# A fused state-space scan and GELU layer: batch 0 prepared in two parts, decays in six ScalarE loads, three masks by ScalarE and GpSimd

## The chip, the core and the metric

The kernel runs on one core of a Trainium2 chip. A core has five engines that run side by side, each working through its own list of instructions in order: TensorE (PE: matrix products, from SBUF into PSUM; PEld is its loading of weights), VectorE (DVE), ScalarE (ACT), GpSimd (POOL), and SyncE (SP), which here only issues DMAs. They wait for each other through semaphores. The metric is device microseconds of one execution, lower is better.

## The reference

First a scan over chunks, as in a state-space model, for 4 batches, 8 heads, 768 steps, head size 32 and state size 16:

```python
log_a = np.log(np.clip(a, 1e-06, 1.0))
for c in range(nc):                          # chunks of 32 steps
    cum = np.cumsum(la, axis=-1)
    L = np.exp(cum[:, :, :, None] - cum[:, :, None, :]) * causal
    M = np.einsum('bhin,bhjn->bhij', Cc, Bc) * L
    y[:, :, sl] = np.einsum('bhij,bhjd->bhid', M, xc) \
        + np.einsum('bhin,bhnd->bhid', Cc, state) * np.exp(cum)[:, :, :, None]
    state = decay_full * state + sum_j(Bc_j * xc_j * np.exp(cum[:, :, -1:] - cum)_j)
```

Then y, as 3072 tokens of 256 features, goes through two products with the tanh form of GELU between them: `out = gelu(y @ w_in) @ w_out`, w_in being 256x2048 and w_out 2048x256.

## The kernel before

The scan is done in 24 chunks of 128 steps (6 for each batch) instead of 32 steps; the result is the same. With r_j, the product of the decays after step j in its chunk, B is multiplied by r and C by 1/r, so that the decay matrix L needs no exponentials: what is left of it is the triangular mask. Chunks are worked in units: chunk 0, chunk 1, and then pairs.

For one unit the steps are these, with the names that the code and the profile use:

- **head, per batch**: clip the decays, scan them backwards for r, transpose r, take 1/r, multiply B and C (`bc`), transpose the products so that head and state lie on the partitions (`bh`, `ch`), and mask C into even and odd heads (`ce`). `pend` holds each chunk's total decay.
- **gram, `f_G`** (line 659): four products of 32 rows per chunk give C·B into `gb`, the four PSUM banks that all units share.
- **mask, `f_M`** (line 669): VectorE multiplies 128x1024 of `gb` by the triangle into `m`, one instruction for each chunk (two half ones for chunk 0).
- **`f_D`** (680): the chunk's contribution to the state, from x and `bn` (B with steps on the partitions again); **`f_S`** and **`f_SP`** (730, 737) on VectorE update the state and spread it by heads (`sp_new`).
- **`f_Y`** (702, 711): y of the unit, in the PSUM bank `yb`; **`f_yev`** (720) moves it to `xm` as bf16.
- **`f_s1`** (757): w_in products into a ring of two PSUM tiles `hp`, 512 columns at a time; **`f_gelu`** (765) on ScalarE moves each to `gT`.
- **`f_s2`** (774): w_out products into the PSUM bank `o_ps`, **`f_oev`** (781, 783) evicts, **`f_store`** (787) stores. The last chunk is split into two column halves (`f_s2h`, 792) in two banks of `gb`, evicted by VectorE and ScalarE.

Batch 0 has a head of its own, which is what the kernel starts with. Its decays come in two loads of 64 rows by 384 steps. Chunk 0 is prepared by itself, from separate small loads of its B and C (`bc0`; line 320), by a TensorE transpose of r (483), two multiplies (576) and two TensorE transposes (583). Chunks 1 to 5 follow from loads of the whole batch (326): 24 small TensorE products (492) transpose r, two multiplies of 768 (595), twelve TensorE transposes (604), ScalarE evictions (458) and VectorE masks (619). For batches 1 to 3 loads and VectorE transposes do it (503 to 553), and six TensorE transposes per batch (625) with a ScalarE eviction of 768 columns (458) make `bn`.

The weights come as fp32 in eight loads of 512 KB (450, 454) and are cast to bf16 by GpSimd and VectorE (460, 462). Their loads, those of x and those of the other batches all are issued by SyncE, in one order, ahead of and between the stores.

The order of instructions on each engine is not written by hand. Every step is a node with an engine, an assumed duration, what it depends on and which ring buffers it takes. A planner (`run_order`) plays these through, picks at each engine the ready node with the lowest priority number (the table `PRIO` gives one for every node), and writes the program in that order. Where it sees TensorE idle before the first w_out product, it puts in matmuls on zeros (`idle`, line 1065), which keep TensorE's clock up; their number is fixed in the program. At run time each engine follows its list in order, whatever the times then are.

Of the kernel before, what the change touches and what calls it, by code (L numbers as in the profile page):

```python
# [31 lines left out]
def run_order(nodes, pools, hop=0.08, same=0.04, idle=None, wait=()):  # L32
# [64 lines left out]
    'f_clip(0, 256)': 308.538, 'f_R(0,)': -15.941, 'f_clip(256, 384)': -339.826, 'f_RT0()': 1159.49,  # L97
    'f_R(1,)': 367.141, 'f_recip0()': -323.896, 'f_mul0(1,)': -323.906, 'f_mul0(0,)': -35.176,
    'f_T0(1,)': 1123.21, 'f_T0(0,)': 1159.5, 'f_ce0()': -138.371, 'f_bh0()': 266.725, 'f_R(2,)': 330.337,
    'f_G(0,)': -91.981, 'f_pe()': -193.992, 'f_RT()': 1125.27, 'f_M(0, 0, 0, 2)': -285.936,  # L100
    'f_M(0, 0, 2, 4)': 367.131, 'f_pp()': 1125.26, 'f_recip()': 468.131, "f_castx(0, 'ACT')": 266.715,
    'f_mul(1,)': -194.002, 'f_pend()': 270.364, 'f_Y(0,)': 1119.78, 'f_yev(0,)': 209.42,
    'f_mul(0,)': -35.176, 'f_T(1,)': 1152.81, "f_wi(0, 0, 2, 'POOL')": 97.158,
    "f_E(0, 1, 'ACT', 21, 64)": 270.354, 'f_T(0,)': 55.447, "f_E(0, 1, 'ACT', 64, 128)": 272.36,
    'f_F(0, 128, 384)': 468.121, 'f_D(0,)': 1170.19, 'f_s1(0, 0)': 1244.43,
    "f_E(0, 0, 'ACT', 21, 64)": -152.035, 'f_F(0, 384, 768)': -343.397, "f_wi(1, 0, 2, 'POOL')": 106.043,
    "f_E(0, 0, 'ACT', 64, 128)": 102.425, 'f_S(0, 0)': -318.328, 'f_G(1,)': 1209.63, 'f_SP(0,)': -323.654,
    'f_gelu(0, 0)': 267.9, 'f_N(0,)': 1123.2, "f_castx(1, 'POOL')": 106.053, 'f_M(1, 0, 0, 4)': -287.074,
    'f_s1(0, 1)': 1244.44, "f_bn(0, 'ACT')": 270.405, 'f_D(1,)': 1119.09, 'f_gelu(0, 1)': 103.579,
    'f_G(2,)': 379.65, "f_wi(2, 0, 1, 'POOL')": -96.227, "f_wi(2, 1, 2, 'DVE')": 244.836,  # L110
    'f_S(1, 0)': 509.234, 'f_Y(1,)': 1167.76, 'f_SP(1,)': -318.348, 'f_s1(0, 2)': -68.513,
    'f_yev(1,)': -185.791, "f_wi(3, 0, 1, 'POOL')": 97.168, "f_wi(3, 1, 2, 'DVE')": -166.728,
# [140 lines left out]
def kernel(  # L253
# [20 lines left out]
    d_ff = moe_w_in.shape[1]  # L274
    d_model = moe_w_in.shape[0]
    n_tokens = batch * S
    NF = d_ff // 128
    UNITS = [[0], [1]] + [[c, c + 1] for c in range(2, NCH, 2)]
    NU = len(UNITS)

# [85 lines left out]
    for t in rr.values():  # L366
        nc.vector.memset(t[:, Q - 1:Q], 1.0)
# [735 lines left out]
```

## Time and profile before

| | us |
|---|---|
| three timed runs | 120.53, 119.59, 119.94 (median 119.94) |
| the profiled execution | 118.98 |
| its span, first to last instruction | 117.0 |
| busy: PE, DVE, ACT, POOL | 111.7, 71.2, 75.3, 18.1 |
| mean granted TensorE clock | 0.995 of full speed |
| fill matmuls (line 1065) in the span | 75, 8.9 us busy |

"Busy" sums the instructions of an engine; TensorE's are pipelined, so that its busy time overlaps itself and says little of what limits it. A line of the timeline gives start, duration, engine, source line, operation, output and inputs, and behind it in brackets the idle time before it with what ended it. A line of the chain gives start, duration and what the last-ending chain of work went through. The profiled execution is one run and the timed ones are others, so a sum of durations is made against 118.98 and its 117.0.

In the head, from 0 to about 20 us, all engines and the DMA are busy in turns: the windows from 4 to 24 us have a DMA share of 0.92 to 1.17. Afterwards TensorE alternates between w_in and w_out products.

### The profile page before, as it was taken

How to read it: one execution, taken by the hardware profiler on the slowest of the kernel's cores; microseconds unless marked ns; L12 is line 12 of the kernel's file. 1: busy time of each engine (PE TensorE's matmuls, PEld its weight loads, DVE VectorE, ACT ScalarE, POOL GpSimd, SP SyncE). 2: the span in 40 equal slices, each digit the busy share in tenths (PEclk: the TensorE clock that was granted, in tenths of full speed). 3: DMA queues.
4: the chain of work that ended last, by engine and by line, in shares of the span. 5: the costliest groups of instructions: out<-in, count | busy, mean ns of one | idle time of the engine just before them, and what ended most of it. 6: DMA issues, size and time to landing. Idle time of an engine off the chain costs nothing.

```text
span 117.0 us, 3536 instructions
## 1 busy us (share of the span) xinstructions
PE 111.7 (96%) x1484; PEld 98.9 (85%) x1484; DVE 71.2 (61%) x161; ACT 75.3 (64%) x145; POOL 18.1 (16%) x38
## 2 busy tenths in 40 slices
PE   5899999999999999999999999999999999999980
PEld 5788778997987897998989899898989899999970
DVE  3787999939699996994999693291919000000100
ACT  4123756795765778687666859667777776676610
POOL 7303735640032003200510000000000000000000
PEclk9999999999999999999999999999999999999998
DMA  2998979968959497579611101101101101111111
GB/s 49 251 287 233 364 180 375 313 153 188 207 137 218 112 210 169 117 186 208 172 46 45 44 7 45 41 12 45 50 0 45 50 0 44 45 50 45 46 47 45
DMA packets 44251, 14.28 MB, mean 122 GB/s; under 512 B 39052, under 2 KB 42700, under 8 KB 44236
## 3 DMA queue, kind: packets, MB, share of 16 engines
q1 hardware_dynamic: 43148, 13.95, 48.4%
q10 hardware_dynamic: 1088, 0.11, 0.7%
q8 instruction: 11, 0.18, 0.6%
q14 instruction: 4, 0.03, 0.1%
HBM read 10.91 MB, written 3.15 MB: 120 GB/s over the span
## 4 chain that ended last, share of the span: by engine, by line
PE 87%; DVE 7%; POOL 2%; issue 1%; ACT 1%; POOLq 0%; DVEq 0%; ACTq 0%
PE hp L757 35%; PE o_ps L774 31%; PE gb L659 3%; PE yb L774 3%; DVE m L669 3%; PE yb L711 3%; PE yb L702 3%; PE o_ps L1065 2%; PE gb L792 2%; DVE ce L619 1%; PE hp L492 1%; PE gb L625 1%; DVE sp_new L737 1%; DVE w_in_sb L462 1%; PE hp L680 1%
## 5 line engine op out<-in xcount | busy, mean ns | idle before, releaser
L765 ACT ACTIVATE gT<-hp 128x512 bf16<-128x512 f32 x96 | 53.6, 596 | 20.0 <-PE hp L757 19.9
L757 PE MATMUL hp<-xm,w_in_sb 128*128 128x256 bf16 (+1 forms) x416 | 53.0, 267 | 0.0
L757 PEld LDWEIGHTS <-w_in_sb 128*128 128x128 bf16 x416 | 42.0, 115 | 3.3 <-issue 2.1
L774 PE MATMUL o_ps<-w_out_sb,gT 128*128 128x256 bf16 x336 | 44.4, 273 | 0.0
L774 PEld LDWEIGHTS <-gT 128*128 128x128 bf16 x368 | 35.8, 98 | 3.6
L669 DVE TENSOR_TENSOR m<-gb,tri 128x1024 bf16<-128x1024 f32 (+1 forms) x25 | 28.5, 1171 | 0.0
L783 DVE COPY o_sb<-o_ps 128x256 f32<-128x256 f32 x1 | 0.4, 425 | 18.5 <-ACT gT L765 18.5
L781 ACT ACTIVATE o_sb<-o_ps 128x256 f32<-128x256 f32 x20 | 7.7, 386 | 4.9 <-ACT gT L765 3.2
L737 DVE SCALAR_TENSOR_TENSOR sp_new<-s_new,pend,bmask 128x256 bf16<-128x256 f32 x20 | 10.3, 526 | 0.3
L1065 PE MATMUL o_ps<-wz 128*128 128x128 bf16 x75 | 8.9, 281 | 1.3 <-DVE warm L364 1.3
L460 POOL CAST x<-xs_t 128x512 bf16<-128x512 f32 x9 | 5.6, 654 | 27.6 <-DMA xs_t<-in_x_dram 18.1
L730 DVE SCALAR_TENSOR_TENSOR s_new<-s_new,pend,hp 128x64 f32<-128x64 f32 x16 | 4.5, 279 | 7.3 <-PE hp L680 4.4
L720 ACT ACTIVATE xm<-yb 128x512 bf16<-128x512 f32 (+1 forms) x13 | 7.3, 563 | 2.4 <-PE yb L711 2.2
L1065 PEld LDWEIGHTS <-wz 128*128 128x128 bf16 x75 | 6.9, 129 | 1.6 <-DVE warm L364 1.3
L711 PE MATMUL yb<-m,x 128*32 128x128 bf16 x192 | 6.3, 223 | 0.0
L702 PE MATMUL yb<-ce,sp_new 128*32 128x128 bf16 x160 | 5.3, 221 | 0.0
L659 PE MATMUL gb<-ce,bh 32*128 32x256 bf16 x96 | 5.2, 282 | 0.1
L533 DVE TENSOR_TENSOR bc<-bc_t,rr 128x192 bf16<-128x192 f32 x12 | 4.6, 435 | 1.0 <-DMA bc_t<-in_C_dram 0.9
L460 POOL CAST w_in_sb<-wf 128x512 bf16<-128x512 f32 x6 | 3.7, 636 | 8.4 <-DMA wf<-in_moe_w_in_dram 8.4
L460 POOL CAST w_out_sb<-wf 128x1024 bf16<-128x1024 f32 x4 | 4.2, 1040 | 2.4 <-DMA wf<-in_moe_w_out_dram 2.4
L711 PEld LDWEIGHTS <-x 128*32 128x32 bf16 x192 | 3.8, 97 | 0.8 <-issue 0.8
L702 PEld LDWEIGHTS <-sp_new 128*32 128x32 bf16 x160 | 2.9, 96 | 1.7 <-issue 1.6
(83 smaller groups left out, 67.3 us busy)
## 6 DMA issues: line engine op xcount, KB each, us to landing
out_dram<-o_sb SPq DMA_DIRECT2D x23, 128.0 KB, 1.8
xs_t<-in_x_dram SPq DMA_DIRECT2D x3, 768.0 KB, 6.6
wf<-in_moe_w_in_dram SPq DMA_DIRECT2D x4, 512.0 KB, 7.0
wf<-in_moe_w_out_dram SPq DMA_DIRECT2D x4, 512.0 KB, 6.4
bc_t<-in_B_dram SPq DMA_DIRECT2D x12, 96.0 KB, 2.8
bc_t<-in_C_dram SPq DMA_DIRECT2D x12, 96.0 KB, 2.3
x_t<-in_x_dram SPq DMA_DIRECT2D x6, 128.0 KB, 7.3
bc_t<-in_C_dram SPq DMA_DIRECT2D x1, 384.0 KB
```

Of the source, the lines that this page charges most:

```text
L460: nc.gpsimd.tensor_copy(out=o, in_=i)
L659: nc.tensor.matmul(out=gb[:, g, 256 * k:256 * k + 256], lhsT=bh_of(gc)[32 * g:32 * g + 32], rhs=ce_of(gc)[32 * g:32 * g + 32], start=True, ...
L669: nc.vector.tensor_tensor(out=MT[gc][:, g0:g1], in0=gb[:, g0:g1, 256 * k:256 * k + 256] .rearrange("p g (e t) -> p g e t", e=2), in1=tri_b ...
L702: nc.tensor.matmul(out=y4[32 * j:32 * j + 32, k, w], lhsT=sp[:, 32 * h:32 * h + 32], rhs=ce_of(gc)[:, h % 2], start=first(j), stop=False, ...
L711: nc.tensor.matmul(out=y4[32 * j:32 * j + 32, k, w], lhsT=X16[u][:, k, 32 * h:32 * h + 32], rhs=m[:, h // 2, h % 2, :], start=first(j), st ...
L720: nc.scalar.activation(xm[:, :, t0:t0 + n * Q].rearrange("p w (c t) -> p c w t", c=n), y4[:, 0:n], AF.Copy)
L737: nc.vector.scalar_tensor_tensor(out=sp_new.rearrange("p (g d) -> p g d", g=4), in0=state[("s", gc)].rearrange("p (o d) -> p o d", o=1).to ...
L757: nc.tensor.matmul(out=hp[:, j * nt:(j + 1) * nt], lhsT=w_in5[:, kc, fi // 4, fi % 4], rhs=xm[:, kc, t0:t0 + nt], start=(kc == 0), stop=(k ...
L765: nc.scalar.activation(gts[u][:, i * per:(i + 1) * per, 0:nt], hps.pop((u, i)).rearrange("p (j t) -> p j t", j=per), AF.Gelu_apprx_tanh)
L774: nc.tensor.matmul(out=ops[gc], lhsT=gts[u][:, fi, tt * Q:(tt + 1) * Q], rhs=w_out_sb[:, fi, :], start=(fi == 0), stop=(fi == NF - 1), ski ...
L781: nc.scalar.activation(o_sb, ops.pop(gc), AF.Copy)
L1065: nc.tensor.matmul(out=zb[:, 0:128], lhsT=wz[:, 0:128], rhs=wz[:, 0:128], start=True, stop=True)
```

## The change

What it does, part by part:

- **Loads of batch 0.** The decays come by chunk, in six loads of 32 rows x 128 steps that ScalarE issues first of all. B and C come in two parts, chunks 0 and 1 and chunks 2 to 5, each part as one load for B and one for C, with no separate load for chunk 0. x comes by chunk, all six of batch 0 ahead of w_out.
- **Head of batch 0.** Both parts go the same way: clip, scan, a VectorE transpose of r, 1/r, four multiplies for each part (B and C, heads 0 to 3 and 4 to 7), products with the identity into fp32 PSUM (line 597), evictions that are masks for C (ScalarE with a scale, or VectorE) and copies for B, TensorE transposes for `bn` and their evictions. The products that transposed r are gone. `par`, `selq` and `mq` are reductions of the identity on VectorE.
- **Masks of chunks 1, 3 and 5.** ScalarE copies the 128x1024 tile of `gb` to `m` (line 694) and GpSimd sets what lies off the triangle to zero in place (697).
- **`bn` of batches 1 to 3.** The six TensorE transposes and the ScalarE eviction are replaced by two regrouping copies for each batch (`bq`, most on GpSimd) and four DMAs from SBUF to SBUF (645).
- **Order and engines.** A table `ENG` now names the engine for copies that several engines can do, so that some evictions of y and of the output and some casts move to VectorE. w_in products of chunks 0 and 1 may alternate, and chunk 1's w_out products go to the other half of chunk 0's PSUM bank, alternating with chunk 0's. `PRIO` is a new table.
- **Last chunk.** Its halves lie in the two tiles of the ring `hp` instead of two banks of `gb`.

```diff
@@ loads and head of batch 0
-    nc.sync.dma_start(out=a_t[0:32], in_=a_half[0])
-    nc.scalar.dma_start(out=a_t[32:64], in_=a_half[1])
-    load_bc0(1, nc.sync)
-    load_bc0(0, nc.scalar)
+    A0 = [(0, 2), (2, CPB)]
+    NP = [32 * (c1 - c0) for c0, c1 in A0]
...
+    def load_a0(c):
+        k = int(c >= A0[1][0])
+        o = 32 * (c - A0[k][0])
+        nc.scalar.dma_start(
+            out=a0t[k][o:o + 32],
+            in_=bass.AP(tensor=a.tensor, offset=a.offset + c * Q, ap=[[S, 32], [1, Q]]))
+
+    def load_bc0(k, i):
+        c0, c1 = A0[k]
+        src = (B, C)[i]
+        nc.sync.dma_start(out=bcq[k][:, i],
+                          in_=bass.AP(tensor=src.tensor, offset=src.offset + c0 * Q * N,
+                                      ap=[[R * N, NP[k]], [S * N, H], [1, R * N]]))
...
+    for c in range(CPB):
+        load_a0(c)
...
+    def f_clip0(k):
+        nc.vector.tensor_scalar(out=a0c[k], in0=a0t[k], scalar1=1e-6, scalar2=1.0, op0=ALU.max, op1=ALU.min)
...
+    def f_mul0(k, i, h0, h1):
+        nc.vector.tensor_tensor(
+            out=bq16(k)[:, i, :, h0:h1], in0=bcq[k][:, i, h0:h1].rearrange("p h (r n) -> p r h n", r=R),
+            in1=(r0T_of(k), q0T[k])[i][:, :, h0:h1].rearrange("p r (h o) -> p r h o", o=1)
+            .to_broadcast([NP[k], R, h1 - h0, N]), op=ALU.mult)
+
+    def f_T0(k, i):
+
+        n = NP[k]
+        T0[(k, i)] = t = next_hp()[:, 0:R * n]
+        for r in range(R):
+            nc.tensor.matmul(out=t.rearrange("q (p r) -> q r p", r=R)[:, r],
+                             lhsT=bq16(k)[:, i, r].rearrange("p h n -> p (h n)"),
+                             rhs=ident[0:n, 0:n], start=True, stop=True)
...
+        if eng == "ACT":
+            nc.scalar.activation(o, i, AF.Copy, scale=par[:, e:e + 1])
+        else:
+            nc.vector.tensor_scalar(out=o, in0=i, scalar1=par[:, e:e + 1], scalar2=None, op0=ALU.mult)
@@ bn of batches 1 to 3
-    def f_N(b):
-        U[b]["n"] = (gb[:, 1] if b else next_hp())[:, 0:S // 2].bitcast(BF16)
-        for c in range(1 if b == 0 else 0, CPB):
-            nc.tensor.transpose(out=U[b]["n"][:, c * 128:(c + 1) * 128],
-                                in_=U[b]["bh"][:, c * Q:(c + 1) * Q], identity=ident)
...
+    def load_bn(b, g):
+
+        d = U[b]
+        if "bn" not in d:
+            d["bn"] = next_bn()
+        nc.sync.dma_start(out=d["bn"][:, 192 * g:192 * g + 192],
+                          in_=d["bq"][32 * g:32 * g + 32].rearrange("p r c n -> p r (c n)"))
@@ masks
+    BYPOOL = range(1, 6, 2)
...
+    def f_MA(u, k):
+
+        gc = UNITS[u][k]
+        MT[gc] = next_m()
+        nc.scalar.activation(MT[gc], gb[:, :, 256 * k:256 * k + 256].rearrange("p g (e t) -> p g e t", e=2), AF.Copy)
+
+    def f_MP(gc):
+        nc.gpsimd.affine_select(out=MT[gc], in_=MT[gc], pattern=[[0, 4], [0, 2], [1, Q]],
+                                compare_op=ALU.is_ge, fill=0.0, base=0, channel_multiplier=-1)
...
+            elif gc in BYPOOL:
+                ma = add("ACT", 1.0, f_MA, u, k, deps=[gn], prio=q + 1)
+                mp = add("POOL", 1.38, f_MP, gc, deps=[ma], prio=q + 1)
@@ last chunk
     def f_s2h(h):
+        ops[("h", h)] = next_hp()[:, 0:128]
...
-            nc.tensor.matmul(out=gb[:, 2 * h, 0:128], lhsT=gts[NU - 1][:, f, Q:2 * Q],
+            nc.tensor.matmul(out=ops[("h", h)], lhsT=gts[len(BLOCKS) - 1][:, f, Q:2 * Q],
```

In the order that the planner makes of it, TensorE's list has 105 fill matmuls instead of 75: 24 at first, then groups of 10, 6, 7, 11, 3, 11 and 11 between the steps of the head, 8 before the first w_in group, and groups of 1 and 5 between the eight w_in groups of chunks 0 and 1. The last one stands behind the eighth of these. On VectorE the last of the second part's multiplies stands behind chunk 1's state update and ahead of chunk 0's masks; on GpSimd chunk 1's select stands behind the casts of x for chunks 0 and 1 and ahead of all casts of weights. In the head of batch 1 all four multiplies of C now come ahead of the first transpose, where two did before, and the stores of chunks 0 and 1 stand between SyncE's DMAs for batch 1's `bn`.

## The prediction

> **What bounds the kernel now.** I read the busy lines first, then the chain that ended last, then the windows of the fill matmuls (line 1065, which multiply zeros only to keep TensorE at work), then the head's timeline engine by engine.
>
> ```profile
> PE 111.7 (96%) x1484; PEld 98.9 (85%) x1484; DVE 71.2 (61%) x161; ACT 75.3 (64%) x145; POOL 18.1 (16%) x38
> PE 87%; DVE 7%; POOL 2%; issue 1%; ACT 1%; POOLq 0%; DVEq 0%; ACTq 0%
> ```
>
> TensorE is busy nearly always and carries 87% of the chain. But part of that is fill:
>
> ```profile
> 0.00:12.00 12.00, 6.48 (x50) 5.21 (x50) 1.00 0.88 209
> 12.00:20.00 8.00, 2.11 (x23) 1.50 (x24) 1.00 0.96 300
> 20.00:30.00 10.00, 0.28 (x2) 0.14 (x2) 1.00 0.91 223
> 30.00:60.00 30.00, 0.00 (x0) 0.00 (x0) 1.00 0.82 169
> ```
>
> These are the windows of line 1065 (busy of PE and PEld with counts, granted clock, DMA share, GB/s). After 20.3 us there is no fill and the clock is 1.00: from there TensorE works through a fixed list. So the end is "when does the last fill end" plus "how much real TensorE work is left", unless a later wait opens. The pieces of the chain that mark this:
>
> ```profile
> 20.21 0.11 PE o_ps L1065 x2
> 32.49 0.35 PE gb L659 x8
> 111.77 1.80 PE gb L792 x32
> 113.66 0.30 DVE o_sb L462
> 114.03 0.28 ACT o_sb L458
> ```
>
> The last fill ends at 20.32, the first gram matmuls of batch 1 (chunks 6 and 7) start at 32.49, the last matmul ends at 113.57, and 3.43 us of eviction and store follow to 117.0. From 20.32 to 113.57 is 93.25 us.
>
> That gram is no free point. VectorE's timeline shows what releases it:
>
> ```profile
> 30.75 0.64 DVE L533 TENSOR_TENSOR bc<-bc_t,rr 128x192 bf16<-128x192 f32 x2 [0.92 <-DMA bc_t<-in_C_dram]
> 31.42 0.38 DVE L543 STREAM_TRANSPOSE ch<-bc 128x192 f32<-128x192 f32 x1
> 31.84 0.55 DVE L553 TENSOR_SCALAR ce<-ch,pari 128x192 int32<-128x192 int32 x2
> ```
>
> VectorE waited 0.92 us for batch 1's C, then scaled, transposed and masked it until 32.39; TensorE took it 0.1 us later. So the load of C is as late as TensorE there: a shorter head alone would wait at this place.
>
> **The change, part by part.**
>
> *TensorE's list.* In the order of the changed kernel the last fill stands right after the eighth w_in group of chunks 0 and 1. What is left there is less than at 20.32 of before: one such group (0.57, "L757 x8"), the Y of chunks 2 and 3 (0.56) and three batches of six transposes (line 625, 0.34 each, replaced by DMAs): 2.15 us. So the end is the same if the last fill ends near 22.5, at equal stalls.
>
> *The head's chain.* I walk it with the rows of before. Six loads of the decays of 0.42 to 0.45 us issue each on ScalarE's queue run from 0.80 to 3.4, the table load (1.28) then ends at 4.7, and ScalarE's first use is after 5. The two loads of the first part land by 3.2 to 3.3 (a_t took 1.9 from issue). VectorE has its constants by about 3.05 (three reductions sized from the 0.255 of line 394, the copy of 0.37 of line 397, one cast of the identity). Clip 0.2, scan 0.42, transpose 0.43 and the state factor 0.15 end at 4.5. Multiplies of 256 elements are not in the trace; between 0.28 (128) and 0.95 (768) a line gives 0.42. Four of them, a reciprocal of 0.37 (between 0.21 for 8 and 0.46 for 48), one copy of 0.28 and a 0.24 end at 7.1; TensorE transposes, ScalarE scales four pieces at 0.28 to 8.7, chunk 1's gram starts at 8.6. ScalarE's copy of its mask tile, 128x1024 from PSUM, is not in the trace: 0.384 (256) and 0.596 (512) give 1.02, so 9.05 to 10.1. GpSimd's select of 1024: 0.292 (128) and 0.450 (256) give 1.38, so 10.2 to 11.6. On VectorE the second part's clip, scan, transpose, factor, three multiplies, a state copy and a reciprocal bring 10.2, a state update 10.5; the last multiply is then due beside the select.
>
> What happens to a VectorE instruction beside GpSimd can be read off:
>
> ```profile
> 15.05 0.42 DVE L462 CAST w_in_sb<-wf 128x512 bf16<-128x512 f32 x1
> 15.99 0.65 POOL L460 CAST w_in_sb<-wf 128x512 bf16<-128x512 f32 x1 [1.50 <-DMA wf<-in_moe_w_in_dram]
> 16.09 0.83 DVE L462 CAST w_in_sb<-wf 128x512 bf16<-128x512 f32 x1
> 20.11 1.04 POOL L460 CAST w_out_sb<-wf 128x1024 bf16<-128x1024 f32 x1 [0.30 <-DMA wf<-in_moe_w_out_dram]
> 20.31 1.12 DVE L737 SCALAR_TENSOR_TENSOR sp_new<-s_new,pend,bmask 128x256 bf16<-128x256 f32 x1
> ```
>
> The cast takes 0.42 alone and 0.83 beside GpSimd, the sp update 0.48 alone (28.26) and 1.12: both end 0.28 after GpSimd's instruction (16.64 and 21.15). So the multiply ends at 11.88 instead of 10.9. Then: two half masks of chunk 0 (1.29) to 13.2, a scaled piece 0.43, sp 0.48, a copy 0.35 to 14.4; D and Y of chunk 1 to 15.05; eight fills to 15.55. From there each pair of w_in groups is a round trip over two PSUM tiles: 0.66 from matmul to gelu, 0.60 gelu, 0.2 back (17.00 to 17.64 to 18.29), 1.46 for a pair; three pairs, 0.6 for a cast of x on ScalarE and one group more: the last fill ends near 21.75. The first w_out product waits for a cast on VectorE (it stands behind chunk 4's mask, from 20.4, 1.2, then 0.42) to 22.1. Weights arrive in time in this walk: 768 KB of x stand ahead of w_out instead of 512, 128 KB fewer of B and C are read, so net 128 KB, 0.5 us at the windows' 250 to 300 GB/s: w_in's last quarter at 16.5 (15.99 before), w_out's first at 19.3 (18.76).
>
> *From there to chunk 6's gram.* 88 matmuls of 0.109 and one Y, 10.1 us, and 0.3 of latencies as before: 32.5. VectorE's side: all six x of batch 0 now stand ahead too, so the same bytes less 128 KB precede C: landing near 30.2. But all four multiplies (1.3) now precede the first transpose (0.38) and masks (0.55): 32.45, 32.55 on TensorE. Both sides meet; I take 32.55 against 32.49.
>
> *After it.* Four w_in matmuls more and four w_out matmuls fewer are done by then, which cancels; two sets of transposes are gone, 0.68. 81.08 becomes 80.4: the last matmul ends at 112.95. The masks of chunks 1, 3 and 5 and the bn evictions moved to or off ScalarE cost nothing here: its idle after 32 us is mostly "gelu waits for PE", 19.9 in all. GpSimd sits idle for 9.5 to 9.9 at a time, which covers the new regrouping copies.
>
> *The tail.* Before, ScalarE's last copy stood behind VectorE's, both in one tile: 114.03, 0.46 after the last matmul. Now the halves have tiles of their own, and ScalarE's needs only about the 0.2 seen from matmul to eviction: 0.25 less.
>
> Sum: 32.55 - 32.49 - 0.68 - 0.25 = -0.87 us. The profiled execution took 118.98 us for a span of 117.0; the sum gives 118.1. The three timed runs have the median 119.94, 0.96 above it; on that scale the forecast is **119.1**. Differences under 1% (1.2 us) hardly count here.
>
> Not shown in the trace: the DMAs from SBUF to SBUF that replace the transposes (below 0: a load that lands ahead costs nothing; above: 2.8 us, the landing of a B load, if all of it is waited for; I take 0, as the copies end near 30.5 and D of chunk 6 is due at 35.7, with four issues of 0.5 and two stores between). The select beside VectorE: from 0 (it does not block) to the 1.4 of its length; I take the 0.95 of one blocked multiply, by the casts' rows. ScalarE's copy of 1024: 0.8 (the bn row of 768) to 1.2.
>
> The Trainium skill, "SBUF — State Buffer", section "Who interferes with whom", says that VectorE with two SBUF inputs, or in its two-port modes, shares a port pair with GpSimd under an exclusive lock, and that the one which comes second blocks for the whole instruction. The two ends at +0.28 agree; no row here shows a select in that place. It speaks against this change, which puts three long selects and more copies beside such VectorE work; taken for every overlap it gives the first rival's time.
>
> **Rivals.**
>
> 1. *VectorE behind GpSimd, everywhere (slower).* Beside the one multiply, three more weight casts on VectorE (+0.42 each) and two or three sp updates (+0.3 to 0.64) stand beside GpSimd's casts and selects between 12 and 20 us: 1.3 + 1.2 = 2.5. It decides once chunk 2's mask ends after 19.5, for then gram 4/5 and the last pair are late: last fill 24.2, end +2.4: 121.5. For: rows above; VectorE is busy 3.9 of 4 us in 12 to 20. Against: masks from PSUM took 1.22 and 2.34 beside GpSimd as without.
> 2. *Nothing blocks and C comes early (faster).* The multiply goes ahead of the select: 0.95 less, last fill 20.8; 1024 fewer small packets let C land at 29.3. Gram at 31.6: 118.2. For: DMA is the limit there, share 0.8 to 1.2. Against: C needs both.
> 3. *C lands as before (the transfer decides).* At 30.75 the gram is at 33.2 whatever the head gains: 119.8. That the change moves only the head, and not the time, is this case.
> 4. *The DMAs for bn are late.* They queue behind two stores that wait for evictions, and GpSimd's copies block on VectorE's multiplies. If the last lands at 38 instead of 35, TensorE stands 2.3 us: 121.4.
>
> **Chances.** Forecast 0.36 (118.5 to 119.6), rival 1 0.15, rival 2 0.22, rival 3 0.17, rival 4 0.10. Faster by over 1% (below 118.74): rival 2 and the forecast's lower third, 0.34. Slower (above 121.14): most of rivals 1 and 4, 0.22. Within: 0.44. The range reaches from rival 2 with the tail's gain doubled and chunk 0's walk 0.5 shorter, 117.4, to rival 1, 121.5.
>
> **What would show it.** Last fill near 21.8; the first mask of chunk 0 right behind a select at 11.6 to 11.9; a VectorE wait for C near 30.2 and gram 6/7 at 32.5; no line of 625's kind after 32; the last copy 0.2 after the last matmul. Wrong: the last fill beyond 23, TensorE gaps between 32 and 60, or the D of chunk 6 released by a DMA.

## The result: slower, and the profile after

| | before | after |
|---|---|---|
| timed runs, median (us) | 120.23 (119.59 to 120.62) | 124.87 (124.50 to 126.77) |
| ratio after/before, 95% interval | | 1.0384 (1.0323 to 1.0446) |
| the profiled execution, and its span | 118.98, 117.0 | 126.77, 125.0 |
| gram of chunks 6 and 7 | 32.49 | 34.55 (forecast 32.55) |
| from it to the last matmul's end | 81.08 | 87.40 (forecast 80.4) |
| from there to the end of the span | 3.43 | 3.05 (forecast 3.18) |

The forecast was 119.1, with a range of 117.4 to 121.5: wrong, in sign too. Ratios, here and below, are to the kernel before, timed beside it, with 95% intervals, and leave out runs that were disturbed on either side, so they need not be the quotient of two medians. The profiled execution is the longest of the four. A second profiled execution of the same kernel (124.84 us, span 123.0) is set beside it where that matters: TensorE ran at half clock for some 3.4 us in both, and what the first has more is mostly longer stands of TensorE (4.66 us after 34 us, against 3.04).

The page of the changed kernel: busy lines, and the engines' shares of the chain that ended last.

```profile
PE 114.0 (91%) x1475; PEld 100.0 (80%) x1475; DVE 72.8 (58%) x176; ACT 75.7 (61%) x147; POOL 19.8 (16%) x38
PE 74%; DVE 8%; DMA 7%; SPq 4%; ACT 3%; issue 1%; ACTq 0%; DVEq 0%
```

TensorE's share of the chain fell from 87% to 74%. DMA (7%) and SyncE's queue (SPq, 4%) are new in it. No engine became the bound; TensorE waits for transfers. The windows of the fill matmuls (now line 1135: busy of PE and PEld with counts, granted clock, DMA share, GB/s):

```profile
0.00:12.00 12.00, 7.62 (x61) 6.11 (x61) 1.00 0.74 160
12.00:20.00 8.00, 3.67 (x37) 2.81 (x37) 1.00 0.99 288
20.00:30.00 10.00, 0.88 (x7) 0.52 (x7) 1.00 1.05 251
30.00:60.00 30.00, 0.00 (x0) 0.00 (x0) 0.94 0.72 147
```

The head is longer (seven fills after 20 us instead of two), and in the first 12 us the DMA moved 160 GB/s instead of 209, which is 0.6 MB less. The clock of 0.94 in the last row is that half clock. TensorE's timeline holds what "equal stalls" in the prediction left out (in brackets: idle time before, and what ended it):

```profile
23.86 0.22 PE L1135 MATMUL o_ps<-wz 128*128 128x128 bf16 x1
...
34.55 0.40 PE L675 MATMUL gb<-ce,bh 32*128 32x256 bf16 x8
...
38.56 0.20 PE L706 MATMUL hp<-x,bn 128*32 128x64 bf16 x1 [0.76 <-DMA bn<-bq]
39.20 0.23 PE L706 MATMUL hp<-x,bn 128*32 128x64 bf16 x5 [0.44 <-DMA bn<-bq]
...
42.36 0.30 PE L728 MATMUL yb<-ce,sp_new 128*32 128x128 bf16 x8 [1.29 <-DVE sp_new L762]
...
53.91 1.35 PE L802 MATMUL o_ps<-w_out_sb,gT 128*128 128x256 bf16 x8 [2.17 <-DVE o_sb L485]
```

Last fill at 24.08 (forecast 21.75), gram at 34.55, and then three stands: 1.20 us at the D of chunk 6, 1.29 at the Y behind it, 2.17 at a w_out group. The second and the third name VectorE, but VectorE was itself waiting. Its timeline:

```profile
41.43 0.23 DVE L495 TENSOR_SCALAR at<-at 128x128 f32<-128x128 f32 x1 [3.62 <-DMA at<-in_a_dram]
41.57 0.22 DVE L753 COPY s_new<-hp 128x64 f32<-128x64 f32 x1
41.82 0.48 DVE L762 SCALAR_TENSOR_TENSOR sp_new<-s_new,pend,bmask 128x256 bf16<-128x256 f32 x1
...
50.24 0.43 DVE L485 CAST x<-xs 128x512 bf16<-128x512 f32 x1 [2.06 <-DMA xs<-in_x_dram]
52.42 0.23 DVE L495 TENSOR_SCALAR at<-at 128x128 f32<-128x128 f32 x1 [1.75 <-DMA at<-in_a_dram]
...
53.47 0.39 DVE L485 COPY o_sb<-o_ps 128x256 f32<-128x256 f32 x1
```

At 41.43 it is the clip of batch 2's decays that waited 3.62 us, and the state copy and `sp_new`, which TensorE needs at once, stand behind it in VectorE's order. At 50.24 and 52.42 it is x of batch 2 and the decays of batch 3; the eviction that TensorE waits for stands behind both. Behind all three stands are DMAs that SyncE issued late. Its timeline (a duration here is the time that issuing took):

```profile
28.72 1.77 SPq L399 DMA_DIRECT2D xs<-in_x_dram  x1
30.59 3.91 SPq L812 DMA_DIRECT2D out_dram<-o_sb  x1
34.59 1.28 SPq L645 DMA_DIRECT2D bn<-bq  x2
35.97 0.54 SPq L812 DMA_DIRECT2D out_dram<-o_sb  x1
36.56 1.19 SPq L645 DMA_DIRECT2D bn<-bq  x2
37.80 0.59 SPq L383 DMA_DIRECT2D at<-in_a_dram  x1
```

The output of that first store had been evicted by 30.24, and yet its issue lasted until 34.50. Only then came `bn`, and the decays of batch 2 at 37.80. The same view of the kernel before:

```profile
27.28 0.47 SPq L353 DMA_DIRECT2D xs_t<-in_x_dram  x1
27.86 5.19 SPq L787 DMA_DIRECT2D out_dram<-o_sb  x2
33.10 0.58 SPq L337 DMA_DIRECT2D at<-in_a_dram  x1
```

There too the queue stood for 5 us behind the load of x (4.71 of the 5.19 us are the first store's, whose output had been evicted by 25.48), but what stood in it were stores that nobody waits for, and the decays went out 4.7 us earlier.

### The profile page after: what moved, and what is told of

Read it like the earlier page. It is cut to its first block, busy times and chain, and to the rows that moved or that the text cites. A ratio compares the mean times of both kernels' runs of the same rounds, so it can differ in the third digit from the quotient of the medians.

```text
span 125.0 us, 3564 instructions
## 1 busy us (share of the span) xinstructions
PE 114.0 (91%) x1475; PEld 100.0 (80%) x1475; DVE 72.8 (58%) x176; ACT 75.7 (61%) x147; POOL 19.8 (16%) x38
## 4 chain that ended last, share of the span: by engine, by line
PE 74%; DVE 8%; DMA 7%; SPq 4%; ACT 3%; issue 1%; ACTq 0%; DVEq 0%
PE hp L782 30%; PE o_ps L802 27%; PE o_ps L1135 4%; DMA at<-in_a_dram 3%; PE yb L802 3%; PE gb L675 3%; PE yb L728 2%; DMA a0t<-in_a_dram 2%; DVE sp_new L762 2%; SPq L645 2%; PE yb L737 2%; DMA wf<-in_B_dram 2%; DVE m L685 1%; PE hp L818 1%; ACT gT L790 1%; SPq L812 1%
## 5 line engine op out<-in xcount | busy, mean ns | idle before, releaser
L802 PE MATMUL o_ps<-w_out_sb,gT 128*128 128x256 bf16 x336 | 46.1, 276 | 2.2 <-DVE o_sb L485 2.2
L685 DVE TENSOR_TENSOR m<-gb,tri 128x1024 bf16<-128x1024 f32 (+1 forms) x22 | 25.3, 1164 | 0.1
L1135 PE MATMUL o_ps<-wz 128*128 128x128 bf16 x105 | 12.2, 283 | 1.3 <-DVE warm L408 1.3
L1135 PEld LDWEIGHTS <-wz 128*128 128x128 bf16 x105 | 9.4, 130 | 1.9 <-DVE warm L408 1.3
L481 ACT ACTIVATE o_sb<-o_ps 128x256 f32<-128x256 f32 x16 | 6.2, 385 | 5.9 <-PE o_ps L802 4.5
L485 DVE COPY o_sb<-o_ps 128x256 f32<-128x256 f32 x5 | 2.1, 417 | 9.6 <-PE o_ps L802 9.6
L481 ACT ACTIVATE xm<-yb 128x512 bf16<-128x512 f32 (+1 forms) x10 | 5.6, 556 | 1.5 <-PE hp L706 1.3
L483 POOL COPY bq<-bc 128x384 bf16<-128x384 bf16 x5 | 2.6, 527 | 21.4 <-DVE bc L528 21.4
L697 POOL TENSOR_SCALAR_AFFINE_SELECT m<-m 128x1024 bf16<-128x1024 bf16 x3 | 3.5, 1172 | 6.9 <-ACT m L694 6.9
L706 PE MATMUL hp<-x,bn 128*32 128x64 bf16 x80 | 3.3, 199 | 1.2 <-DMA bn<-bq 1.2
```

The lines of the kernel that those rows point to most:

```text
L481: nc.scalar.activation(o, i, AF.Copy)
L685: nc.vector.tensor_tensor(out=MT[gc][:, g0:g1], in0=gb[:, g0:g1, 256 * k:256 * k + 256] .rearrange("p g (e t) -> p g e t", e=2), in1=tri_b ...
L697: nc.gpsimd.affine_select(out=MT[gc], in_=MT[gc], pattern=[[0, 4], [0, 2], [1, Q]], compare_op=ALU.is_ge, fill=0.0, base=0, channel_multip ...
L802: nc.tensor.matmul(out=ops[gc], lhsT=gts[v][:, fi, tt * Q:(tt + 1) * Q], rhs=w_out_sb[:, fi, :], start=(fi == 0 and gc != 1), stop=(fi == ...
L1135: nc.tensor.matmul(out=zb[:, 0:128], lhsT=wz[:, 0:128], rhs=wz[:, 0:128], start=True, stop=True)
```

## The experiments

Theory A: the loss is made from 34 us on, by SyncE's queue: `bn` and batch 2's loads stand behind the load of batch 1's x, VectorE and TensorE behind them. Theory B: the loss is the later head. Each variant is the changed kernel with the order of all other instructions kept. Where a diff says `move`, one entry of the planned order is put behind another one.

### e0_after: the changed kernel again

> The changed kernel as it is, for a profile that can be set beside the variants. Both theories: 124.5 to 125.2 us. Theory A (the loss is made between 32 and 56 us, by SyncE's order of DMAs) expects to see TensorE stand at the D of chunk 6 (1.2 us, for bn), at the Y behind it (1.3, for sp_new) and at the first w_out group near 54 (2.2, for o_sb), 4.7 us in all; theory B (the loss is the later head, 2.0 to 2.3 us up to the gram of chunks 6 and 7) expects those stands to be peculiar to the first trace and the gram of chunks 6 and 7 near 34.5 again.

Ratio 1.0475 (1.0334 to 1.0616), from two runs. Gram of chunks 6 and 7 at 34.27, last matmul's end 85.77 later. The stands are there again: 1.05 and 0.44 at the D, 1.55 at w_out. At the Y there was none, because TensorE came late to it: it had run at half clock since 39.8. The stands are no accident of the first trace. The late gram is there again too, which is what theory B expects; this run does not tell the theories apart by the time.

### e1_early_a: the decays of batches 2 and 3 loaded early

```diff
+    move("load_a(2,)", "load_a(1,)")
+    move("load_a(3,)", "load_a(2,)")
```

> The decays of batches 2 and 3 (64 KB each) are loaded right behind those of batch 1, ahead of the stores and of the DMAs for bn, and nothing else is changed. Theory A: VectorE no longer waits 3.6 us for batch 2's decays near 41 nor 1.75 for batch 3's near 52, so TensorE's stands of 1.3 (sp_new) and 2.2 (o_sb) go: 3.5 less, 121.0 to 122.0 us. The stand of 1.2 at the D of chunk 6 stays. Theory B: TensorE is late from the head on and VectorE's waits lie beside it: 124.5 to 125.0, or 0.2 more for 128 KB ahead of batch 1's C.

Ratio 1.0294 (1.0217 to 1.0372), 123.71 us: 1.2 us less, not 3.5. VectorE's waits for decays were gone, as expected, and with them TensorE's stand at the Y; the one at w_out was 0.97. But in the profiled run (125.40 us, the longest of the five) B and C of batch 1, which now stand behind the decays, came late: SyncE issued C from 29.12 instead of 23.09, VectorE waited 3.01 us for B, TensorE 2.13 for `ce`, and the gram of chunks 6 and 7 moved to 37.54. One late load had been put in the place of another.

### e2_bn_gpsimd: the bn DMAs on GpSimd's queue

```diff
-        nc.sync.dma_start(out=d["bn"][:, 192 * g:192 * g + 192],
+        nc.gpsimd.dma_start(out=d["bn"][:, 192 * g:192 * g + 192],
```

> The twelve DMAs for bn are issued by GpSimd behind its regrouping copies instead of by SyncE between the stores. Theory A: the D of chunk 6 no longer waits for bn (1.2 less), and SyncE issues batch 2's decays 2.5 us earlier (35.3 instead of 37.8), which cuts VectorE's wait of 3.6 to 1.1 and takes most of the 1.3 at the Y: 2.0 to 2.5 less in all, 122.0 to 122.7 us. If what holds SyncE is the store ahead (3.9 us up to 34.5) and not the bn DMAs, only 1.2 goes: 123.4. Theory B: 124.5 to 125.

Ratio 1.0187 (1.0100 to 1.0274), 122.14 us: 2.7 less, as theory A had it. The stand at the D is gone and the one at the Y is 0.54; the third is still there with 2.3. The gram stayed at 34.66. By the ratios about half of the loss goes by changing who issues twelve small DMAs.

### e10_stores_last: what holds the queue

```diff
+    move("f_store(1,)", "load_a(2,)")
+    move("f_store(0,)", "f_store(1,)")
```

> The changed kernel, with the stores of chunks 0 and 1 moved in SyncE's order from among the four bn DMAs to behind the load of batch 2's decays; bn and decays stay on SyncE. It tells apart what holds bn. If it is the stores' waits for evictions (rival 4 as predicted): bn goes out when GpSimd's copies end, near 32.8, and the decays at 35.3, as with bn on GpSimd's queue: 2.0 to 2.7 us less, 122.2 to 122.9. If it is the load of batch 1's x (768 KB in 6144 pieces of 128 bytes), behind which SyncE can issue nothing until about 34.5, whatever comes next: bn is then the one that is held, goes out at 34.5 to 37.0 and the decays follow at 37.0 instead of 37.9: 0.5 to 1.2 less, 123.7 to 124.4.

Ratio 1.0389 (1.0303 to 1.0475), 125.83 us: no gain at all, and so neither of the two times expected. The order of events was that of the second alternative. SyncE's timeline of this kernel, with the first bn DMA cut out of its group by a narrow window:

```profile
29.93 1.53 SPq L399 DMA_DIRECT2D xs<-in_x_dram  x1
32.68 2.77 SPq L645 DMA_DIRECT2D bn<-bq  x1
37.44 0.59 SPq L383 DMA_DIRECT2D at<-in_a_dram  x1
```

GpSimd's second regrouping copy ended at 32.65, so nothing that the program waits for was missing. Still the issue of this one DMA took 2.77 us, until 35.45, when the x load issued at 29.93 (6.8 us to landing) had a good microsecond left. Whatever stands behind that load is held, be it a store or `bn`. The mechanism that rival 4 named, stores waiting for evictions, is not what holds it. Which limit in the queue it is, the traces do not show. The gain of 0.5 us or more did not come because the decays went out only 0.36 earlier (37.44 instead of 37.80), and in this trace the head was later (gram at 35.44) and the third stand longer (3.25).

### e3_bn_pe and e11_bn_pe: bn by TensorE, as before

```diff
+    def f_N(b):
+        U[b]["n"] = t = next_hp()[:, 0:S // 2].bitcast(BF16)
+        for c in range(CPB):
+            nc.tensor.transpose(out=t[:, c * 128:(c + 1) * 128],
+                                in_=U[b]["bh"][:, c * Q:(c + 1) * Q], identity=ident)
+    put("N1", lambda: f_N(1), "f_G(4,)")
+    put("bn1", lambda: f_bn(1), "f_gelu(3, 2)")
...
```

In e3 the transposes of batches 2 and 3 fell into a PSUM tile that a state update had yet to read, so those updates worked on other values and e3 computes something else; e11 places them two or three steps later.

> bn of batches 1 to 3 comes as in the kernel before, from six TensorE transposes per batch and one ScalarE copy of 768 columns; the two regrouping copies and the four DMAs per batch are gone. TensorE has 3 times 0.34 = 1.0 us more of work. Theory A: the stand at the D of chunk 6 goes (1.2), SyncE is 2.5 us ahead, which takes most of the 1.3 at the Y: 1.5 less net, 123.0 us. Theory B: nothing was lost by the DMAs, so the transposes cost their 1.0: 125.5 us.

> The changed kernel, with bn of batches 1 to 3 by six TensorE transposes each and a ScalarE copy of 768 columns, as in the kernel before; no regrouping copies and no DMAs for bn; all else as changed, batch 2's and 3's decays on SyncE too. TensorE has 1.0 us more of work. Theory A (the bn DMAs are late and make SyncE late): 122.3 to 123.0, in spite of that 1.0. Theory B (the loss is in the head): 125.5 to 126.

e3: ratio 1.0207 (1.0128 to 1.0287). e11: 1.0230 (1.0175 to 1.0285), 122.89 us. Theory A's number in both: giving TensorE 1.0 us more of work makes the kernel 2 us faster. The part of the change that was to save 0.68 us cost about 2 net.

### e4_two_fixes: bn and the late decays on GpSimd's queue

```diff
-        nc.sync.dma_start(out=d["bn"][:, 192 * g:192 * g + 192],
+        nc.gpsimd.dma_start(out=d["bn"][:, 192 * g:192 * g + 192],
@@ load_a
-        nc.sync.dma_start(out=at[b], in_=bass.AP(tensor=a.tensor, offset=a.offset + b * H * S - K0[b] * Q,
+        (nc.sync if b == 1 else nc.gpsimd).dma_start(out=at[b], in_=bass.AP(tensor=a.tensor, offset=a.offset + b * H * S - K0[b] * Q,
@@ order
+    move("load_a(2,)", "f_wo(3, 0)")
+    move("load_a(3,)", "load_a(2,)")
```

> The bn DMAs issued by GpSimd, and with them the loads of the decays of batches 2 and 3, issued by GpSimd behind its last weight cast; the rest as changed. Theory A: the stands that the first of these left (0.5 at the Y for sp_new, 2.3 at w_out for o_sb, both behind VectorE's waits for decays) go too: 122.1 - 2.8 = 119.3 us; the gram of chunks 6 and 7 stays at 34.0 to 34.7, and from there to the last matmul 80.4 to 81 us, as forecast. Theory B (the stands lie beside a TensorE that is late anyway): 122.1.

Ratio 0.9997 (0.9944 to 1.0050): the whole loss is gone within the noise, without a change in the head. With 120.95 us, beside a kernel before that had 120.70 in these rounds, it is 1 us or more short of the 119.3 expected: a wait of 2.93 us on VectorE for batch 2's x (47.48) was left, and with it 1.29 of the stand at w_out.

### e12_head_only: the head mended, the queue not

```diff
-            for _ in range(n):
+            for _ in range(n + (10 if t0 < 2 else 0)):
+    move("f_mul0(1, 1, 4, 8)", "f_mul0(1, 1, 0, 4)")
```

> The changed kernel with only its head mended: ten more fill matmuls before the first state factor, and the last multiply of the second part ahead of chunk 1's state update. SyncE's list is as changed. Theory A (SyncE's queue behind the load of batch 1's x decides from 34 us on): the first w_in group comes 1 to 2 us earlier, but the load of x goes out near 28.8 and batch 2's decays near 37.8 as before, so TensorE stands longer at the D of chunk 6 and the Y: 124.3 to 124.9. Theory B (the head is the loss): 1.5 to 2.0 less, 123.0.

Ratio 1.0318 (1.0250 to 1.0387), 124.44 us: 0.4 less, theory A's number. Batch 2's decays went out at 37.48, and the stands were 0.8, 1.3 and 1.7. But the test is weaker than meant. In the profiled run the head was not earlier: the first w_in group began at 16.75, against 17.97 and 16.16 in the two traces of the changed kernel, then the granted clock fell (0.74, 0.50 and 0.91 in the windows of 2 us from 16 on), the last fill ended at 24.10 and the gram of chunks 6 and 7 came at 34.57. What speaks against theory B is above all e4, which left the head alone and lost the loss.

### e13_evict_act: the eviction and the cast off VectorE

```diff
+    seq[pos("f_oev(5,)")][1] = lambda: f_oev(5, "ACT")
+    seq[pos("f_castx(7,)")][1] = lambda: f_castx(7, "POOL")
```

> The changed kernel, with the eviction of chunk 5's output on ScalarE instead of VectorE and the cast of chunks 12 and 13's x on GpSimd instead of VectorE, both at their places in the order; loads as changed. If the third stand (1.6 to 3.3 us at w_out near 53) comes about because the eviction stands on VectorE behind a cast that waits for x and a clip that waits for decays: it goes, 1.5 to 2.5 less, 122.5 to 123.4. If TensorE would stand there anyway, for the gram or the Y that need the same late loads: the stand only moves to a later line, 124.5.

Ratio 1.0247 (1.0186 to 1.0307), 123.22 us: 1.6 less. VectorE still waited 3.95 us for batch 3's decays there (51.07), but the eviction no longer stood behind. What is left of the third stand, on TensorE:

```profile
52.42 1.07 PE L782 MATMUL hp<-xm,w_in_sb 128*128 128x256 bf16 x8 [0.85 <-DVE s_new L755]
```

So this stand had two causes in series, the late loads and the table `ENG` that put a cast and an eviction on VectorE behind them. The prediction did not look at the second.

### e5_two_loads, e6_fills, e7_masks_dve: parts of the head, on e4

```diff
@@ e5: load_a0 (n is the number of chunks of the part)
-        nc.scalar.dma_start(
-            out=a0t[k][o:o + 32],
-            in_=bass.AP(tensor=a.tensor, offset=a.offset + c * Q, ap=[[S, 32], [1, Q]]))
+        if o == 0:
+            nc.scalar.dma_start(
+                out=a0t[k],
+                in_=bass.AP(tensor=a.tensor, offset=a.offset + c * Q, ap=[[Q, n], [S, 32], [1, Q]]))
@@ e6: idle
-            for _ in range(n):
+            for _ in range(n + (10 if t0 < 2 else 0)):
@@ e7: f_MA (and f_MP issues nothing)
-        nc.scalar.activation(MT[gc], gb[:, :, 256 * k:256 * k + 256].rearrange("p g (e t) -> p g e t", e=2), AF.Copy)
+        nc.vector.tensor_tensor(out=MT[gc], in0=gb[:, :, 256 * k:256 * k + 256]
+                                .rearrange("p g (e t) -> p g e t", e=2), in1=tri_b, op=ALU.mult)
```

> On the kernel with the two fixes (bn and late decays issued by GpSimd), the decays of batch 0 come in two ScalarE loads (64 and 128 rows) instead of six. In the program each of the DMAs of SyncE and ScalarE waits for the one eight places before it; with six decay loads and two of B and C in front, the first load of x is the ninth and waits for a decay load to land (2.5 us), and so on. Theory C (this makes the whole stream of loads late, 0.6 MB behind the kernel before at 12 us): x goes out at 1.7 instead of 2.5 and the first w_in load at 5.0 instead of 5.9, the gram of chunks 6 and 7 comes 0.7 to 1.0 earlier than with six loads, and the time is 0.7 to 1.0 less. Theory D (the head is late by TensorE's clock and the chain of steps): clip starts 0.5 earlier at most, nothing else moves: 0 to 0.3 less.

Ratio 1.0123 (1.0038 to 1.0208): slower than e4. The two loads take the place of six, but the first lands later. VectorE's first clip in e4, then in e5:

```profile
3.83 0.22 DVE L553 TENSOR_SCALAR a0c<-a0t 64x128 f32<-64x128 f32 x1 [1.20 <-DMA a0t<-in_a_dram]
```

```profile
4.71 0.22 DVE L555 TENSOR_SCALAR a0c<-a0t 64x128 f32<-64x128 f32 x1 [2.09 <-DMA a0t<-in_a_dram]
```

It therefore tells nothing between theories C and D.

> On the kernel with the two fixes, ten more fill matmuls in the first group (34 instead of 24), which close TensorE's gap of 0.9 us before the first state factor (4.0 to 4.9 us). Theory D (TensorE's matmuls take twice as long until 5, 9 or 13 us, by chance from run to run, because of that gap): fills of 0.06 us from about 5.5 us on in every run, steps of the head 1 to 2 us earlier, and the time 1 to 2 us less and steadier. Theory C (w_out's and C's landing decides when TensorE goes on): the head's first part is earlier, but TensorE then waits for casts of w_out and for ce, and the gram of chunks 6 and 7 and the time gain 0.5 or less.

Ratio 0.9939 (0.9894 to 0.9983), the fastest version here and the only one with an interval below 1. In this trace the rate changed as theory D said: eleven fills took 1.28 us start to start in the first trace after and take 0.72 here. These are their rows, first of the changed kernel, then of e6, each with the gram that follows them:

```profile
9.71 1.35 PE L1135 MATMUL o_ps<-wz 128*128 128x128 bf16 x11
10.99 0.40 PE L675 MATMUL gb<-ce,bh 32*128 32x256 bf16 x4
```

```profile
8.07 0.79 PE L1135 MATMUL o_ps<-wz 128*128 128x128 bf16 x11
8.79 0.29 PE L675 MATMUL gb<-ce,bh 32*128 32x256 bf16 x4
```

Chunk 1's gram came 2.2 us earlier than in the first trace after, and the last fill ended at 22.2. But the gram of chunks 6 and 7 stood at 34.58, where TensorE waited 1.0 for `ce`, and the gain over e4 is 0.6%, theory C's number, with intervals that overlap. That the gap was the reason for the slow matmuls is not shown: of the traces with the same ten more fills, e8, e12 and e14 have them slow again behind the first state factor (ten fills in 1.25 us, against 0.73 in e6 and e9). The time was not steadier either: e6's runs lie between 119.22 and 123.27.

> On the kernel with the two fixes, the masks of chunks 1, 3 and 5 are done by VectorE in one step of 1.24 us at the place where ScalarE's copy stood; no copy and no select. If the selects hurt (VectorE's multiply and sp update wait 0.9 and 1.6 us beside them, and the casts of w_in that the third and fourth w_out loads wait for stand behind the first select): 0.5 to 1.5 us less. If VectorE is the bound of the head (3 times 1.24 more on it up to 25 us): 1 to 2 us more. If neither: within 0.4.

Ratio 1.0088 (1.0042 to 1.0134), against 0.9997 for e4, with intervals that overlap a little. The masks of the title by themselves may be worth up to 0.9%, or 1 us, to the changed kernel, which is not clear of the noise; they are not what made it slow.

### e8_pool_decays, e9_mul_first, e14_best: on e6

```diff
@@ e8: load_a0 (the loop over chunks 2 to 5 stands behind GpSimd's constants)
-        nc.scalar.dma_start(
+        (nc.gpsimd if k else nc.scalar).dma_start(
@@ e9: order
+    move("f_mul0(1, 1, 4, 8)", "f_mul0(1, 1, 0, 4)")
@@ e14: order
+    seq[pos("f_oev(5,)")][1] = lambda: f_oev(5, "ACT")
+    seq[pos("f_castx(7,)")][1] = lambda: f_castx(7, "POOL")
```

> On the kernel with the two fixes and ten more fills (119.7 us): the four loads of the second part's decays are issued by GpSimd behind its constants instead of by ScalarE at the start, so that they take none of the eight places that the DMAs of SyncE and ScalarE go through. Theory C (those loads hold up the stream of x and w_in): first x out at 1.9 instead of 2.5, first w_in at 5.0 instead of 5.9, the gram of chunks 6 and 7 0.7 to 1.0 earlier and the time 0.5 to 1.0 less, 118.7 to 119.2 us. If the stream is not what decides: 119.7, or up to 0.5 more as the second part's decays land near 6 instead of 4.5 us.

Ratio 1.0025 (0.9991 to 1.0059): no gain over e6, rather 0.9% lost. The first w_in load went out at 5.13 instead of 5.74, but by 12 us no more bytes had moved. By this trace the eight places are not what makes the stream late.

> On the kernel with the two fixes and ten more fills (119.7 us): the last of the second part's multiplies stands ahead of chunk 1's state update on VectorE, so that it is over before GpSimd's first select begins. The prediction charged 0.95 us for this multiply beside the select. If that is lost time at the end: chunk 0's mask begins 0.6 to 1.0 earlier and the time is 0.5 to 1.0 less, 118.7 to 119.2. If the loads of w_out and of batch 1's C decide when TensorE goes on: the mask is earlier and the time is 119.7 all the same.

Ratio 0.9982 (0.9929 to 1.0035): no gain. The profiles show why it tested little: in e6 the multiply began at 10.22 together with the select and took its 0.42; the select took 1.37 instead of the 1.10 of the first trace after and the 1.18 of e9. It looks as if here the select was the one that waited.

> The two fixes on GpSimd's queue (bn, decays of batches 2 and 3), ten more fills, and the eviction of chunk 5 and the cast of chunks 12 and 13 off VectorE. The kernel with the first three had 119.7 us and a stand of 0.7 left at w_out for o_sb. If that goes: 119.0, 1% below the kernel before. If the head's loads decide: 119.7.

Ratio 0.9962 (0.9916 to 1.0009): no measurable gain over e6 or over the kernel before (the median of all its twelve runs is 121.09, that of the kernel before 120.46). Its profiled execution (119.68 us, span 118.0) is the clean one of this study, with no stand after 34.43. Its TensorE timeline:

```profile
34.43 0.40 PE L675 MATMUL gb<-ce,bh 32*128 32x256 bf16 x8 [0.63 <-DVE ce L548]
...
112.89 1.95 PE L818 MATMUL hp<-w_out_sb,gT 128*128 128x128 bf16 x32
```

From 34.43 to 114.84 are 80.41 us, and 3.16 from there to the end.

## Why the prediction was wrong, point by point

- **The step that failed** is the term "the DMAs from SBUF to SBUF ... I take 0", and with it "at equal stalls": the sum has no TensorE stand behind the gram of chunks 6 and 7. The trace has 4.66 us of them. The prediction counted when the copies end, what an issue costs and two stores between, and not that SyncE's list stands for about 4 us behind 768 KB of x, nor which loads stand behind `bn`. 1.20 us of the stands are `bn`'s own, and the 1.29 at the Y are in the main what `bn` made late (0.54 in e2); together that is about half of the loss (ratio 1.0384, and 1.0187 in e2). The third stand is not `bn`'s (2.34 in e2): it comes from x and decays that SyncE issues late and from the cast and the eviction that `ENG` put on VectorE behind them (e4, e13). The row to read was in the profile of before, 5.19 us for two stores behind the load of x.
- **Its signs of being wrong** all came: the last fill beyond 23, TensorE gaps between 32 and 60, the D of chunk 6 released by a DMA.
- **Rival 4** had the right place (the D of chunk 6 released by a DMA, `bn` landing after 38) and was given 0.10. Its cause was wrong (not the stores' evictions, e10) and it ended too early: it priced 2.3 us at one D and not what is queued on VectorE behind the next load.
- **From the gram to the last matmul, 80.4.** Right as a sum of work: e14, with no stand, has 80.41. The six transposes per batch were worth their 0.68. Wrong as a forecast of this kernel, which has 87.40: 4.66 us in the three stands, and of the rest most in matmuls at half clock (below).
- **The tail, 0.25 less.** Right: ScalarE's last copy began at 122.04, 0.1 after the last matmul's end, and e14 has 3.16 instead of 3.43.
- **The last fill at 21.75.** It came at 24.08, with the clip at 4.0 instead of 3.3 (the loads landed later than "by 3.2 to 3.3") and fills at 0.117 us each until 13.6. In e6, where TensorE ran at full rate from 5 us on, it is 22.2, and in the second trace, with the full rate from 9.4, 22.43. So the walk was off by half a microsecond or more, and the rest goes with the slow matmuls, which differ from trace to trace; the kernel before had them too (eight fills in 1.04 us at 9.01).
- **The gram at 32.55.** It is at 34.55 and 34.27 in the two traces of the changed kernel, and from 33.30 (e13) to 37.54 (e1) in the variants. The prediction had two sides meet there, and both were late. TensorE's came 10.47 us behind the last fill, as forecast (10.1 and 0.3), so the fill's lateness comes through. VectorE's had `ce` ready at 33.92, against 32.39 before. TensorE began the gram at 34.55 without waiting for it: in this trace TensorE's side decided, by 0.6 us. In e6, e9 and e14, whose last fills ended at 21.4 to 22.6, TensorE waited 0.6 to 1.1 us for `ce` and the gram was at 34.43 to 34.58 all the same: there VectorE's side decided. VectorE's timeline of the changed kernel:

```profile
27.86 0.43 DVE L485 CAST w_out_sb<-wf 128x512 bf16<-128x512 f32 x1 [2.04 <-DMA wf<-in_moe_w_out_dram]
28.20 0.64 DVE L495 TENSOR_SCALAR at<-at 128x128 f32<-128x128 f32 x1
...
29.80 1.18 DVE L528 TENSOR_TENSOR bc<-bc,at 128x192 bf16<-128x192 f32 x4
...
31.88 1.17 DVE L528 TENSOR_TENSOR bc<-bc,rr 128x192 bf16<-128x192 f32 x4
...
33.37 0.55 DVE L548 TENSOR_SCALAR ce<-ch,pari 128x192 int32<-128x192 int32 x2
```

  What it waits for is the last of w_out, whose cast stands ahead of batch 1's head in VectorE's order (before, VectorE had no such cast after 21 us), and neither B nor C. In e14 it waits for these as well:

```profile
27.34 0.43 DVE L485 CAST w_out_sb<-wf 128x512 bf16<-128x512 f32 x1 [1.23 <-DMA wf<-in_moe_w_out_dram]
27.69 0.63 DVE L495 TENSOR_SCALAR at<-at 128x128 f32<-128x128 f32 x1
...
29.81 1.18 DVE L528 TENSOR_TENSOR bc<-bc,at 128x192 bf16<-128x192 f32 x4 [0.55 <-DMA bc<-in_B_dram]
...
32.30 1.18 DVE L528 TENSOR_TENSOR bc<-bc,rr 128x192 bf16<-128x192 f32 x4 [0.45 <-DMA bc<-in_C_dram]
```

  In both traces clip, B and C are 1.1 to 2.7 us later than before (clip 25.53, B 27.40, C 30.75). The prediction looked at C alone, near 30.2. By 28 us 6.4 MB had moved, against 6.8. Why the stream is slower between 4 and 8 us (179 to 214 GB/s in the changed kernel, e4, e6, e8 and e14, 304 before) is not settled. The loads there are small pieces of B, C and x, where before it was w_in, but no run here changed their order.
- **The select beside VectorE.** Right in kind: the multiply at 12.60 took 1.31 and ended 0.28 after the select, `sp_new` x2 took 2.07 beside the second one. Selects took 1.10 to 1.28 and not 1.38. Wrong in weight: in e6 the multiply went unblocked and the gram of chunks 6 and 7 was no earlier, and in e7, without the copies and selects, the time was no shorter.
- **Rivals 1 to 3** all argued about the head. e4 shows that this wasn't where the loss was made.

So the 8.0 us between the two profiled executions are +2.06 up to the gram, +6.32 from there, -0.38 in the tail. Of the 4.6 us between the medians, the queue and what stands behind it account for all: with `bn` and the late decays off it, the time is that of before, within 0.6%. What stays open is the gram's lateness, which can eat up what the rest of the change saves behind it. By the profiles e14 is 1.0 us longer than before (+1.94 up to the gram, -0.67 and -0.27 behind it), by the ratio it is not longer: the profiled execution of before was a short one, 118.98 against a median of 120.23. How late the gram is in a typical pair of runs these profiles don't tell.

## What to carry to other kernels

Before a step is replaced by DMAs on a queue, list everything in that queue ahead and behind, and look in the old profile for the row where its issue already lasts long: what was free for stores is not free for operands. Then follow each load that comes later to the engine that waits for it in order, and see what else stands behind that instruction; two of the three stands here named VectorE, and neither was VectorE's work. And a head that is made shorter moves the end only as far as the next late load lets it (e6 against e4: the last fill 1.1 us earlier, the gram no earlier).

## What the runs showed of the hardware that was not expected

- **A long load holds the queue.** Behind 768 KB in pieces of 128 bytes (6144 of them), the next DMA of the same queue took 2.77 to 4.71 us to issue with nothing left to wait for (e10: 32.68 to 35.45; after: 30.59 to 34.50; before: 27.86 to 32.57). Whether the bytes or the number of pieces does it, and what the loads ahead of x add, no run here separates. Four DMAs on GpSimd's queue took 2.31 us in the same time in e2, and landed in time for the D.
- **TensorE's full rate comes at different times in programs that differ little.** The ten fills behind the first state factor took 1.25 us in eleven of the sixteen traces of the changed kernel and its variants, and 0.73 in five (e1, e3, e6, e9 and e13). The eleven fills right ahead of chunk 1's gram took 1.35 in the first trace after and 0.79 in the second. The gap before the first state factor does not settle it: of the eleven traces with it three have 0.73, of the five with ten more fills two. The granted clock reads 1.00 in all of that time, so the column does not show it. The Trainium skill, "TensorE: Matmul & The Clock Gate", section "Part 1: The HAM clock gate", has the rate doubled after a busy window of about 3.4 us that runs free of the kernel's start; the five traces, with 0.73 from 5.1 to 5.5 us on, agree with that in kind, and no run here shows why the others took longer.
- **A stand can cost more than its length.** Behind 2.17 us of standing the first trace of after shows the clock at half for 3.4 us (an estimate from the two shares below; windows with the busy times and counts of all engines; the last three figures are the granted clock, the DMA share and GB/s):

```profile
54.00:56.00 2.00, 2.00 (x13) 1.51 (x13) 1.97 (x5) 0.00 (x0) 0.00 (x0) 0.62 0.83 211
56.00:58.00 2.00, 2.00 (x12) 1.44 (x11) 2.00 (x5) 1.19 (x2) 0.00 (x0) 0.52 0.55 127
```

  The second trace has 0.50 from 40 to 42, behind stands of 1.05 and 0.44, and e10 has 0.51 from 54 to 56 behind 3.25; e2, with a stand of 2.3, has 1.00 throughout. At half rate up to 1.7 us are lost each time, by estimate.
- **A load's shape can outweigh the number of loads.** Of two loads whose sources have an outermost dimension of 2 and 4, the first landed 0.9 us later than the first two of six whose outermost dimension is 32 (clip at 4.71 and 3.83), though the two were issued in 1.72 us and the six in 3.18. The Trainium skill, "DMA: Bandwidth & Descriptors", section "Why a DMA increments its semaphore by 16 and not by 1", says that a transfer is spread over as many engines, up to 16, as divide the outermost sizes of both sides; by that rule it would be, as an estimate, 2 and 4 engines instead of 16. No run here shows the engines one by one.
- **Blocking goes by who comes first.** The multiply that started with the select at the same moment (e6, 10.22) took its own 0.42 and the select 1.37, 0.2 to 0.3 more than in e9 and the first trace after; where the select was first (after) the multiply took 0.9 more.
